# A fused attention and feed-forward kernel: staged loads, V from the padding of K, one GpSimd addition for two, and a forecast that gives VectorE a second tile

## The chip, the cores and the metric

The kernel runs on one core of a Trainium2 chip. The metric is device time in microseconds (us) of one execution; the kernel before takes 809.61 us, the median of 13 runs (808.16 to 811.75). The engines of the core work side by side, each through its own list of instructions in order, and wait for one another by semaphores: TensorE (PE in the profile), VectorE (DVE), ScalarE (ACT), GpSimd (POOL) and SyncE (SP), which here only starts transfers.

## The reference

One transformer layer on 2048 rows of 640 numbers in bf16: attention with 32 query heads of 20 columns that all share one K and one V head, then a gated feed-forward part with 1536 inner columns.

```python
def _A_ref(x, wq, wk, wv, wo):          # x is layernorm(A_x), 2048 x 640
    q = (x @ wq).reshape(B, S, H, Dh)   # then heads first; H = 32, Dh = 20
    k = x @ wk                          # 2048 x 20
    v = x @ wv                          # 2048 x 20
    scores = einsum("bhqd,bkd->bhqk", q, k) * (Dh ** -0.5)
    p = softmax(scores)
    return einsum("bhqk,bkd->bhqd", p, v) (heads joined) @ wo

def _B_ref(x, w_gate, w_up, w_down):    # x is layernorm(h)
    return (gelu(x @ w_gate) * (x @ w_up)) @ w_down

h = x + _A_ref(layernorm(x), ...)
h2 = h + _B_ref(layernorm(h), ...)
```

## The kernel before

**Who decides the order.** The program is written by a planner that runs before anything is emitted. `_Plan.commit` puts an operation at the end of one engine's list, with a planned start, a cost and a latency after which others see its result. The main loop at the end of the kernel takes the engine that is free earliest in planned time and asks that engine's function (`pe_decide`, `act_decide`, `dve_decide`, `pool_decide`, `sp_decide`) for its next operation. Costs and latencies are constants in ns, such as `c_act(n) = n/1.2 + 51` or `POOL_ADD = 635`. They set the order alone: on the chip each engine goes through its finished list, waiting on semaphores where data must come first. An operation that was planned too early therefore holds everything behind it on its engine.

**Scores.** The 2048 query rows are cut into chunks of two tiles of 128 rows (the last two chunks of one), and a chunk into units of several groups of four heads, so that a unit has 512 query columns for each of four heads. For a unit and one tile of 128 keys, `issue_qk` emits a pack: four matmuls, one for each 32-row group of the array, that fill four PSUM banks of 128 x 512 scores. There are 512 packs, 2048 score tiles. A head has 20 columns but takes 32 rows of its group: `wk4` and `wq_pad` hold the weights with 12 zero columns after each 20, so K and the queries carry 12 zero rows, and all four groups of `kT4` hold the same K.

**Exponentials.** `issue_qk` decides how many of the four tiles, `n`, go to DVE; the rest go to ACT. ACT computes the exponential from PSUM into a slot of `pa` (line 1375), one bank (128x512) or two neighbouring banks (128x1024) in one instruction. With n = 1 ACT gets one single and one pair, with n = 2 two singles (since `PAIR2` is 0), with n = 0 two pairs. DVE instead makes a 16-bit number whose bit pattern, read as bf16, approximates the exponential (line 1438). To lower the error it takes three copies of it, of which two are shifted by the integers 42 and 85 (`CH_SHIFT`, the two chord additions), and multiplies each with a V of its own weight (`v_ext`, `CH_W`). So a tile on DVE needs two integer additions and three value matmuls, a tile on ACT one value matmul. The additions wait in `pend[1]` and `pend[2]`; `pool_decide` gives one at a time to POOL (`do_adds`, line 1416), on pairs of 16-bit numbers as int32. DVE may take some too (line 1410), several tiles at once. `pd` has eight slots for such tiles, each with all three copies.

**The rule for n** (line 989): none in the first four packs (`npack`); in a burst, when ACT is planned busy for over 3 us, four or two; none when DVE's planned load `Dv` is over `TH0` = 1500 ns; two when it is under `TH2` = 0, which does not occur; otherwise one.

**Banks.** PSUM has eight. Banks 0 to 5 take scores, bank 6 or 7 holds the unit's accumulated output, and the other serves projections and feed-forward pieces; while no such piece is ready or running, `spare_ok` lends it to scores. Until all K tiles are there (`kv_left`), pieces may also use banks 4 and 5.

**The start.** The loads of x go out from SP, those of wk, wq (two halves) and wv from ACT (line 330). Each tile of x gets its statistics on DVE (line 391), a power on POOL (line 411), a reciprocal and the normalising on DVE (lines 415 and 460), then a transpose: on PE for tiles 0 and 1, by transfer from SP for the others (line 452). `kv_job` then makes K with five accumulating matmuls and V with five more per tile. `flex_copy` tasks take both out of the bank, on DVE or ACT, and free it. POOL copies wk into `wk4` (line 886) and wq into `wq_pad` (`wq_copy`, line 892). A unit's first pack needs its query projection (`q_job`).

**The rest.** Output projection, second layernorm and feed-forward pieces of finished chunks fill PE's gaps between packs, and the last chunk's are the tail.

Of the kernel before, what the change touches and what calls it, by code (L numbers as in the profile page):

```python
# [178 lines left out]
class _Job:  # L179


    __slots__ = ("name", "prio", "pieces", "bank", "then", "seq", "pos", "gate")

    def __init__(self, name, prio, pieces, then, gate=None):
        self.name = name
        self.prio = prio
        self.pieces = pieces
        self.then = then
        self.bank = None
        self.pos = 0  # L190
        self.gate = gate


def bass_sequential_preLN__grouped_kv_mqa__glu_gated_geglu__prompt_kernel(
# [75 lines left out]
    zz = sb("zz", [P, 32], BF16)  # L270
    shifts = sb("shifts", [P, 2], I32)
# [41 lines left out]
    POOL_ADD = 635.0  # L313
    ADD_MIN = 1
# [8 lines left out]
    PAIR2 = 0  # L323
    ADDW = 50.0
# [4 lines left out]
    def load(eng, o, i, key, cost=480.0, lat=2300.0):  # L329
        return plan.commit(eng, (lambda e: e.dma_start(o, i)), cost, lat, writes=key, dma=True)  # L330

    load("sp", xh[:, 0, :], x_view[:, 0, :], [("x", 0)], lat=2000)
    load("act", wk_sb[:], cview(A_wk), ["wk"], lat=2500)
    load("sp", xh[:, 1, :], x_view[:, 1, :], [("x", 1)], lat=2200)
    load("act", wq_stage[:, :, 0:HALF], cview(A_wq)[:, :, 0:HALF], [("wqs", 0)], lat=4000)
    load("sp", xh[:, 2:4, :], x_view[:, 2:4, :], [("x", 2), ("x", 3)], lat=2800)
    load("act", wv_sb[:], cview(A_wv), ["wv"], lat=2500)
    load("sp", xh[:, 4:8, :], x_view[:, 4:8, :], [("x", t) for t in range(4, 8)], lat=4000)
    load("act", wq_stage[:, :, HALF:D], cview(A_wq)[:, :, HALF:D], [("wqs", 1)], lat=4000)
    load("sp", xh[:, 8:12, :], x_view[:, 8:12, :], [("x", t) for t in range(8, 12)], lat=5000)  # L340
    load("sp", xh[:, 12:16, :], x_view[:, 12:16, :], [("x", t) for t in range(12, 16)], lat=6000)
# [40 lines left out]
    def ln_half(ln, t, h, prio, then):  # L382
# [8 lines left out]
        dve(lambda e: e.bn_stats(stats[:, ln, t, 6 * h:6 * h + 6], xh[:, t, h * HALF:(h + 1) * HALF]), 356, [key],  # L391
            [("st", ln, t, h)], prio, c)

    def ln_group(ln, tiles, prio, done):
# [15 lines left out]
        def c3(op):  # L410
            task(("pool",), lambda e: e.tensor_tensor(ln_denb[:, ln, sl], ln_veb[:, ln, sl], halfc[:, 0:n], ALU.pow),  # L411
                 1010, L_POOL, [("veb", kk), "halfc"], [("den", kk)], prio, c4)
# [9 lines left out]
        def norm(t):  # L422
# [33 lines left out]
            tk = _Task(("dve",), None, 310, L_DVE, keys + [("lr", kk)], [], prio, then, gate)  # L456
# [65 lines left out]
    def kv_job(tiles):  # L522
# [3 lines left out]
        for c in range(NC_D):  # L526
            pieces.append((mm(lambda b: bank(b, n), wk4[:, c, :], xn1T[:, c, t0 * P:t0 * P + n],
                              c == 0, c == NC_D - 1), c_mm(n), [("xn1T", t) for t in tiles] + ["wk4"]))
        for i, t in enumerate(tiles):
            for c in range(NC_D):  # L530
                pieces.append((mm((lambda i: lambda b: ps[:, b * 512 + 384 + i * 32:b * 512 + 384 + i * 32 + Dh])(i),
                                  xn1T[:, c, t * P:(t + 1) * P], wv_sb[:, c, :], c == 0, c == NC_D - 1),
                               c_mm(32), [("xn1T", t), "wv"]))

        def then(b):
            cnt = [0]

            def fin(op):
                cnt[0] += 1
                if cnt[0] == 2:  # L540
                    free_bank(b)

            def kfin(op):
# [3 lines left out]
                fin(op)  # L547

            flex_copy(kT4[:, t0 * P:t0 * P + n], bank(b, n), n, [("b", b)], [("k", t) for t in tiles], 0.4, kfin)
            nt = len(tiles)  # L550
            vi = ps[:, b * 512 + 384:b * 512 + 384 + 32 * nt].rearrange("p (t e) -> p t e", t=nt)[:, :, 0:Dh]

            def vfin(op):
                fin(op)
# [330 lines left out]
    wk4v = wk4[:].rearrange("p c (r e) -> p c r e", r=4)[:, :, :, 0:Dh]  # L885
# [762 lines left out]
```

## Time and profile before

| | |
|---|---|
| Median of 13 runs | 809.61 us |
| The profiled execution's own time | 811.45 us |
| Its span (first to last instruction) | 809.7 us |
| ACT busy | 762.0 us (94%) |
| PE busy | 693.3 us (86%) |
| POOL busy | 638.4 us (79%) |
| DVE busy | 573.9 us (71%) |
| Score tiles on DVE | 535 of 2048 |
| Additions on POOL | 1036 |
| First exponential starts | 15.80 us |

In lines of groups, the first number after the bar is the busy time of the group in us, then the mean duration of one in ns, then the idle time of the engine before them and what ended it. In lines of the timeline the first two numbers are start and duration in us, and a bracket gives the idle time before and its releaser. In lines by stretch, the stretch and its length are followed by busy time and number of instructions of PE, weight loads (PEld), DVE, ACT and POOL, then the granted TensorE clock, the share of DMA time and GB/s.

### The profile page before, as it was taken

What the parts mean: (1) busy time and instruction counts of PE and PEld (TensorE: products, weight loads), DVE (VectorE), ACT (ScalarE), POOL (GpSimd) and SP (SyncE); (2) the same over time, 40 slices, a digit from 0 to 9 for tenths busy, and PEclk for the clock granted to TensorE, in tenths of its full rate; (3) what the DMA queues carried; (4) which work ended last, traced back from release to release, by engine and by line L of the source; (5) the groups of instructions that cost most, each with busy time, mean ns of one, the idle gap of its engine ahead of it and who ended that gap; (6) DMA issues with size and microseconds to landing.
All of it is one profiled execution on the core that took longest, in us unless ns stands there. A gap on an engine that the chain in (4) does not pass through costs nothing.

```text
span 809.7 us, 30789 instructions
## 1 busy us (share of the span) xinstructions
PE 693.3 (86%) x13435; PEld 334.2 (41%) x13435; DVE 573.9 (71%) x1060; ACT 762.0 (94%) x1054; POOL 638.4 (79%) x1096
## 2 busy tenths in 40 slices
PE   4777778889889897889978898898988899888998
PEld 2432223444334443345434443354433454344457
DVE  7865557776687766776677766777667766777854
ACT  3699999999999999999999999999999999999991
POOL 5488788888888888888888888888888778888860
PEclk9899999999999999999999999999999999999999
DMA  7590000100100000000000000100000000000000
GB/s 202 81 341 3 2 1 18 20 2 11 25 20 3 2 19 19 19 2 3 18 19 18 2 11 16 29 3 2 19 18 19 2 2 19 19 18 11 11 19 18
DMA packets 40293, 22.01 MB, mean 27 GB/s; under 512 B 31328, under 2 KB 38880, under 8 KB 40160
## 3 DMA queue, kind: packets, MB, share of 16 engines
q1 hardware_dynamic: 37536, 19.18, 9.5%
q8 instruction: 107, 1.75, 0.9%
q10 hardware_dynamic: 2624, 0.87, 0.5%
q14 instruction: 26, 0.21, 0.1%
HBM read 10.21 MB, written 2.62 MB: 16 GB/s over the span
## 4 chain that ended last, share of the span: by engine, by line
ACT 77%; PE 14%; DVE 5%; DMA 2%; issue 1%; POOL 0%; ACTq 0%
ACT pa L1375 73%; PE ps L1037 4%; PE ps L1116 4%; PE ps L498 4%; PE ps L494 3%; DVE pd L1438 2%; ACT gbuf L819 2%; DMA gbuf<-in_A_wq_dram 1%; DVE osb L1143 1%; ACT L1375 1%; ACT L819 1%; DVE xn_tmp L460 1%; DMA xn1T<-xn_tmp 1%; DVE stats L391 0%; PE ps L1240 0%
## 5 line engine op out<-in xcount | busy, mean ns | idle before, releaser
L1375 ACT ACTIVATE pa<-ps 128x512 bf16<-128x512 f32 (+1 forms) x1009 | 713.4, 951 | 17.9 <-PE ps L1037 17.6
L1416 POOL TENSOR_TENSOR pd<-pd,shifts 128x256 int32<-128x256 int32 x1036 | 614.3, 615 | 130.7 <-DVE pd L1438 119.0
L1438 DVE TENSOR_SCALAR pd<-ps 128x512 uint16<-128x512 f32 x535 | 365.5, 689 | 204.8 <-PE ps L1037 198.7
L1116 PE MATMUL ps<-pd,v_ext 128*32 128x512 bf16 x1605 | 274.0, 387 | 34.5 <-DVE osb L1143 18.7
L1116 PE MATMUL ps<-pa,v_ext 128*32 128x512 bf16 x1513 | 265.1, 386 | 3.6 <-DVE pd L1438 2.2
L1037 PE MATMUL ps<-qT,kT 32*128 32x512 bf16 x2048 | 204.4, 384 | 58.3 <-DVE pd L1438 24.8
L1037 PEld LDWEIGHTS ps<-qT,kT 32*128 32x128 bf16 x2048 | 61.0, 91 | 216.2 <-DVE pd L1438 143.0
L1116 PEld LDWEIGHTS ps<-pd,v_ext 128*32 128x32 bf16 x1605 | 73.5, 95 | 94.5 <-ACT pa L1375 32.7
L1116 PEld LDWEIGHTS ps<-pa,v_ext 128*32 128x32 bf16 x1513 | 70.0, 95 | 47.6 <-issue 33.5
L498 PE MATMUL ps<-wd_sb,gbuf 128*32 128x320 bf16 x1344 | 64.1, 301 | 0.0
L498 PE MATMUL ps<-xn2T,wg_sb 128*32 128x256 bf16 (+1 forms) x1748 | 63.4, 272 | 0.7
L498 PE MATMUL ps<-xn2T,wu_sb 128*32 128x256 bf16 x1680 | 61.2, 277 | 2.9 <-DVE gbuf L836 2.9
L498 PEld LDWEIGHTS ps<-xn2T,wg_sb 128*32 128x32 bf16 x1748 | 42.0, 96 | 19.8 <-issue 12.2
L498 PEld LDWEIGHTS ps<-xn2T,wu_sb 128*32 128x32 bf16 x1680 | 41.9, 97 | 18.8 <-issue 9.1
L498 PE MATMUL ps<-xn1T,wq_pad 128*32 128x256 bf16 (+1 forms) x1440 | 47.9, 265 | 0.0
L498 PEld LDWEIGHTS ps<-wd_sb,gbuf 128*32 128x32 bf16 x1344 | 32.9, 96 | 22.8 <-issue 11.1
L498 PEld LDWEIGHTS ps<-xn1T,wq_pad 128*32 128x32 bf16 x1440 | 32.7, 97 | 14.7 <-issue 10.7
L836 DVE TENSOR_TENSOR gbuf<-ps,gbuf 128x512 bf16<-128x512 f32 x48 | 32.7, 682 | 6.6 <-PE ps L494 6.6
L391 DVE BATCH_NORM_STATS2 stats<-xh 128x6 f32<-128x320 bf16 x64 | 30.0, 483 | 3.0 <-DMA xh<-in_A_x_dram 2.6
L799 DVE CAST gbuf<-ps 128x512 bf16<-128x512 f32 x42 | 29.0, 690 | 0.2 <-PE ps L498 0.2
L498 PE MATMUL ps<-wo_sb,onT 128*32 128x320 bf16 x600 | 27.1, 300 | 0.0
L411 POOL TENSOR_TENSOR ln_denb<-ln_veb,halfc 128x2 bf16<-128x2 bf16 (+1 forms) x18 | 12.6, 701 | 15.4 <-DVE ln_veb L407 14.0
(68 smaller groups left out, 334.3 us busy)
## 6 DMA issues: line engine op xcount, KB each, us to landing
out_dram<-xh SPq DMA_DIRECT2D x16, 160.0 KB, 1.8
xh<-in_A_x_dram SPq DMA_DIRECT2D x3, 640.0 KB, 9.5
wg_sb<-in_B_w_gate_dram SPq DMA_DIRECT2D x1, 1920.0 KB, 10.4
wu_sb<-in_B_w_up_dram SPq DMA_DIRECT2D x1, 1920.0 KB, 14.8
wd_sb<-in_B_w_down_dram SPq DMA_DIRECT2D x1, 1920.0 KB, 19.5
gbuf<-in_A_wq_dram ACTq DMA_DIRECT2D x2, 400.0 KB, 9.1
wo_sb<-in_A_wo_dram SPq DMA_DIRECT2D x1, 800.0 KB, 4.9
xh<-in_A_x_dram SPq DMA_DIRECT2D x2, 160.0 KB, 2.8
```

The costliest lines, as they stand in the source:

```text
L391: dve(lambda e: e.bn_stats(stats[:, ln, t, 6 * h:6 * h + 6], xh[:, t, h * HALF:(h + 1) * HALF]), 356, [key], [("st", ln, t, h)], prio, c)
L411: task(("pool",), lambda e: e.tensor_tensor(ln_denb[:, ln, sl], ln_veb[:, ln, sl], halfc[:, 0:n], ALU.pow), 1010, L_POOL, [("veb", kk), "h ...
L494: return e.matmul(o(b), l, r, start=st, stop=sp)
L498: ins = e.matmul(o(b)[a, :], l[:, a], r, start=st, stop=sp, tile_position=(0, 32 * j))
L799: dve(lambda e: e.tensor_copy(o, i), c_dve(n * k), [("b", bk)], ks, 1.0, fin)
L819: task(("act",), (lambda v: lambda e: e.activation(v, v, ACT.Gelu_apprx_tanh))(v), ("gelu", c_act(n * (f1 - f0))), L_ACT, ks, ks, 1.0, (la ...
L836: dve(lambda e: e.tensor_tensor(o, i, o, ALU.mult), c_dve(n * k), [("b", bk)] + ks, ks, 1.0, fin)
L1037: ins = e.matmul(bank(b), kT4[32 * r:32 * r + 32, kt * P:(kt + 1) * P], qT[32 * r:32 * r + 32, s, :], start=True, stop=True, tile_position ...
L1116: ins = e.matmul(ps[32 * r:32 * r + 32, ab * 512:(ab + 1) * 512], v_ext[:, it["kt"], it["w"], :], it["ap"], start=st, stop=(j in ends), ti ...
L1375: op = plan.commit("act", lambda e: e.activation(dst, src, ACT.Exp, scale=SM_SCALE), cost, L_ACT, [("b", b0 + i) for i in range(n)], [("pa ...
L1416: return e.tensor_tensor(pd32[:, w, h], pd32[:, 0, h], shifts[:, w - 1:w].to_broadcast([P, 256 * k]), ALU.add)
L1438: op = plan.commit("dve", lambda e: e.tensor_scalar(pd[:, 0, s * 512:(s + 1) * 512], bank(b), CH_A, CH_B, ALU.mult, ALU.add), c_dve(512), ...
```

## The change

There are four parts and some new constants.

1. *Loads.* `load` can wait for earlier data. SP now starts x tile 0, x tile 1 and wv; then, when tile 0 has landed, x tiles 2 and 3, 4 to 7, 8 to 11, the second half of wq, and x tiles 12 to 15. ACT starts wk and the first half of wq. The planned landing times are later than before. A wq copy may go to ACT while no pack has been issued.
2. *V from the padding rows.* POOL copies the 20 columns of wv, 10 and 10, into the zero columns of the first two 32-column groups of `wk4`. The K projection then brings V, transposed, in rows 20 to 29 of those groups of `kT4`. The query's rows are zero there, so the scores do not change. After the K copy, one matmul for each tile with `vsel` (columns 20 to 29 and 52 to 61 of the identity) takes V out into the same bank, transposed back. The five V matmuls of a tile are gone. `wk4` is now ready only when both wk and wv have come.
3. *Both additions at once.* When the same slot stands first in `pend[1]` and `pend[2]`, POOL adds both shifts in one instruction (`add_both`) on 2 x 256 int32 numbers.
4. *Two tiles to DVE.* n is also 2 if DVE's load is under 400 ns, fewer than six additions wait, and `stall` forecasts that the pack with n = 2 leaves ACT ready more than 300 ns earlier than with n = 1. `stall` sorts the times at which banks come free, from the ACT and DVE queues with the new pack added, takes the one that makes the fourth bank free and compares the next pack's arrival with the end of ACT's work.

The constants `HEADN`, `HEAD2` and `NP0` leave the conditions in which they stand as they were. The planned costs of statistics, normalising and the power change from 356, 310 and 1010 to 395, 420 and 780.

```diff
+    POOL_ADD2 = 1200.0
+    SP2 = 1
+    SP2D = 400.0
+    SP2P = 3
+    SP2G = 300.0
...
+    load("sp", xh[:, 0, :], x_view[:, 0, :], [("x", 0)], 2000)
+    load("act", wk_sb[:], cview(A_wk), ["wk"], 2500)
+    load("sp", xh[:, 1, :], x_view[:, 1, :], [("x", 1)], 2300)
+    load("act", wq_stage[:, :, 0:HALF], cview(A_wq)[:, :, 0:HALF], [("wqs", 0)], 4500)
+    load("sp", wv_sb[:], cview(A_wv), ["wv"], 3000)
+
+    load("sp", xh[:, 2:4, :], x_view[:, 2:4, :], [("x", 2), ("x", 3)], 3200, [("x", 0)])
+    load("sp", xh[:, 4:8, :], x_view[:, 4:8, :], [("x", t) for t in range(4, 8)], 5800)
+    load("sp", xh[:, 8:12, :], x_view[:, 8:12, :], [("x", t) for t in range(8, 12)], 8500)
+    load("sp", wq_stage[:, :, HALF:D], cview(A_wq)[:, :, HALF:D], [("wqs", 1)], 10000)
+    load("sp", xh[:, 12:16, :], x_view[:, 12:16, :], [("x", t) for t in range(12, 16)], 12800)
...
-        for i, t in enumerate(tiles):
-            for c in range(NC_D):
-                pieces.append((mm((lambda i: lambda b: ps[:, b * 512 + 384 + i * 32:b * 512 + 384 + i * 32 + Dh])(i),
-                                  xn1T[:, c, t * P:(t + 1) * P], wv_sb[:, c, :], c == 0, c == NC_D - 1),
-                               c_mm(32), [("xn1T", t), "wv"]))
...
+                jb = _Job(("v", t0), 0.5, vpieces, vthen)
+                jb.bank = b
+                bank_owner[b] = jb.name
+                active.append(jb)
...
+            vpieces.append((mm((lambda i: lambda b: ps[:, b * 512 + i * 32:b * 512 + i * 32 + Dh])(i),
+                               kT4[:, t * P:(t + 1) * P], vsel[:], True, True), c_mm(32), [("k", t), "vsel"]))
...
+    ptask(lambda e: e.tensor_copy(wk4r[:, :, 0:2, Dh:Dh + VH], wv_sb[:].rearrange("p c (r e) -> p c r e", r=2)), 160,
+          ["wv", "wk4z"], ["wk4v"], 1.05)
...
+    def stall(t, n, fb):
+
+        free = [t] * (len(fb) - 4)
+        ta = plan.free["act"]
+        for kind, tl in act_q:
+            ta = max(ta, tl[0]["vis"]) + c_act(512 * len(tl))
+            free += [ta + L_ACT] * len(tl)
+        td = plan.free["dve"]
+        for x in dve_q:
+            td = max(td, x["vis"]) + 600.0
+            free.append(td + L_DVE)
+        free += [r for r, b in free_banks(t)[1] if b not in fb]
+        vis = t + 445.0
+        ta = max(ta, vis)
+        for k in ((2, 2), (1, 2), (1, 1))[n]:
+            ta += c_act(512 * k)
+            free += [ta + L_ACT] * k
+        td = max(td, vis)
+        for _ in range(n):
+            td += 600.0
+            free.append(td + L_DVE)
+        free.sort()
+        return max(0.0, free[3] + 460.0 - ta)
...
-        elif Dv < TH2:
+        elif Dv < TH2 or (SP2 and Dv < SP2D and len(pend[1]) + len(pend[2]) < 2 * SP2P
+                          and stall(t, 1, fb) + 1382.0 - stall(t, 2, fb) - 956.0 > SP2G):
             n = 2
...
+    def add_both(t):
+
+        x = pend[1].pop(0)
+        y = pend[2].pop(0)
+        s = x["slot"]
+        h = slice(s * 256, (s + 1) * 256)
+
+        def fn(e):
+            return e.tensor_tensor(pd32[:, 1:3, h], pd32[:, 0, h].unsqueeze(1).to_broadcast([P, 2, 256]),
+                                   shifts[:].unsqueeze(2).to_broadcast([P, 2, 256]), ALU.add)
+        op = plan.commit("pool", fn, POOL_ADD2, L_POOL, [("pd", 0, s), ("sh", 1), ("sh", 2)],
+                         [("pd", 1, s), ("pd", 2, s)], at=t)
+        x["add"](1, op)
+        y["add"](2, op)
...
+            if pend[1] and pend[2] and pend[1][0]["slot"] == pend[2][0]["slot"] and pend[1][0]["at"] <= t + 20:
+                add_both(t)
+                return True
```

## The prediction

> **What bounds the kernel now.** I read the page's busy shares first, then the chain of waits, then busy time by stage, then the costliest groups, and last the start in the timeline. The page's first part and the lines by share of the chain:
>
> ```profile
> PE 693.3 (86%) x13435; PEld 334.2 (41%) x13435; DVE 573.9 (71%) x1060; ACT 762.0 (94%) x1054; POOL 638.4 (79%) x1096
> ACT 77%; PE 14%; DVE 5%; DMA 2%; issue 1%; POOL 0%; ACTq 0%
> ```
>
> ScalarE is busiest and carries 77% of the chain, 73% of it exponentials. An average hides stages, so the next view is busy time in four stretches (columns: PE, PEld, DVE, ACT, POOL):
>
> ```profile
> 0.00:15.80 15.80, 5.24 (x143) 3.84 (x147) 11.25 (x41) 3.85 (x8) 8.87 (x28) 1.00 0.89 240
> 15.80:40.00 24.20, 17.14 (x532) 10.57 (x524) 20.96 (x72) 15.64 (x18) 11.94 (x25) 0.86 0.55 80
> 40.00:785.00 745.00, 649.06 (x12471) 300.94 (x12469) 532.02 (x926) 735.75 (x1019) 617.00 (x1044) 1.00 0.08 21
> 785.00:809.70 24.70, 21.83 (x302) 18.86 (x299) 9.66 (x21) 6.76 (x10) 0.62 (x2) 1.00 0.04 15
> ```
>
> From 40 to 785 us ACT is idle for 9 us only: there time is won only by taking exponentials off ACT. Before 40 us ACT is idle for 20.5 us (12.0 before the first exponential at 15.80, 8.6 after it): there earlier data wins time. The tail is dependent work that the change does not touch. The groups that the rest is priced from (mean ns of one; idle before it and its releaser):
>
> ```profile
> L1416 POOL TENSOR_TENSOR pd<-pd,shifts 128x256 int32<-128x256 int32 x1036 | 614.3, 615 | 130.7 <-DVE pd L1438 119.0 <-DVE ln_r L415 2.0
> L1375 ACT ACTIVATE pa<-ps 128x1024 bf16<-128x1024 f32 x504 | 587.9, 1168 | 4.3 <-PE ps L1037 4.3
> L1375 ACT ACTIVATE pa<-ps 128x512 bf16<-128x512 f32 x505 | 369.8, 735 | 13.6 <-PE ps L1037 13.4
> L1438 DVE TENSOR_SCALAR pd<-ps 128x512 uint16<-128x512 f32 x535 | 365.5, 689 | 204.8 <-PE ps L1037 198.7
> ```
>
> Of 2048 score tiles DVE takes 535. DVE and POOL stand idle for 199 and 119 us waiting for the next score pack, not for lack of capacity. A mean ACTIVATE overlaps its neighbours, so I take pitches: in the chain 60 ACTIVATEs (30 packs of one single and one pair) take 41.89 us, 1.396 us a pack; two pairs take 1.94 us and four 3.77, so a pair is 0.915 and a single 0.481.
>
> The start, on POOL and DVE (bracket: idle before and releaser):
>
> ```profile
> 3.21 0.89 DVE L391 BATCH_NORM_STATS2 stats<-xh 128x6 f32<-128x320 bf16 x2 [1.01 <-DMA xh<-in_A_x_dram]
> 5.65 0.55 POOL L411 TENSOR_TENSOR ln_denb<-ln_veb,halfc 128x1 bf16<-128x1 bf16 x1 [1.56 <-DVE ln_veb L407]
> 6.91 0.49 DVE L391 BATCH_NORM_STATS2 stats<-xh 128x6 f32<-128x320 bf16 x1 [1.35 <-DMA xh<-in_A_x_dram]
> 8.04 0.52 POOL L892 COPY wq_pad<-gbuf 128x400 bf16<-128x400 bf16 x1 [1.84 <-DMA gbuf<-in_A_wq_dram]
> 8.62 0.14 DVE L415 RECIPROCAL ln_r<-ln_denb 128x1 f32<-128x1 bf16 x1
> 13.88 0.98 POOL L892 COPY wq_pad<-gbuf 128x400 bf16<-128x400 bf16 x2 [1.96 <-DMA gbuf<-in_A_wq_dram]
> wv_sb<-in_A_wv_dram ACTq DMA_DIRECT2D x1, 25.0 KB, 8.7
> ```
>
> The power for tile 0 is done at 6.20, but its reciprocal runs at 8.62: the written-out order put statistics of tiles 2 and 3 ahead of it, whose data came at 6.9. The power for tile 1 stood behind a wq copy whose data came at 8.04 (it ran at 8.51). Loads later than forecast hold the in-order engines.
>
> [...] the 25 KB of wv needed 8.7 us among the x and wq loads while wk, first in its queue, needed 2.7. [...] the pitches give 0.915 - 0.481 = 0.434.
>
> **The change part by part.**
>
> *Two tiles to DVE.* A pack now costs ACT single + pair, 1.396 us; with two tiles on DVE it costs two singles, 0.962. One moved tile is worth 0.43 us of ACT. When does the rule fire? It asks for DVE load under 400 ns, fewer than six pending additions and a forecast gain over 300 ns, that is an added ACT stall under 126 ns. I work this with the plan's own times for a pack in which six banks hold scores. Let ACT's backlog be A when the pack issues. The old pair's two banks come free at A + 310, DVE's first at 445 + 600 + 150 = 1195, ACT's first new single at A + 478 + 310 = A + 788; the next pack needs the fourth of these, so its tiles arrive at A + 788 + 460 while ACT runs dry at A + 956: stall 292, over 126, and no move. With a seventh bank the fourth is the 1195, and the move is allowed once A exceeds 573. So it fires only where bank 6 or 7 is lent to scores, which `spare_ok` allows when no projection or feed-forward piece is ready. Counted over the timeline's PE rows, 138 of 512 packs have no such matmul from 0.3 us before to 1.1 us after their start, about 54 of these before 147 us, where feed-forward work begins. A unit has 16 packs; its first and last three or so are barred (two open units, or fewer than three tiles left): 138 x 10/16 = 86 eligible.
>
> How many of the 86? POOL alone allows a share f with (1 + f) x 1.18 = 1.396 - 0.43 f: f = 0.13, 11 tiles. If DVE, with about 0.7 us free a pack, takes the surplus additions (eight single ones averaged 278 ns), it is full near f = 0.45, 39 tiles. I take 22. Of the 0.43 I deduct 0.12 for the stall that the rule tolerates: 22 x 0.31 = 6.8 us. Ends: 0 and 39 x 0.43 = 16.8. A moved tile adds two value matmuls; eight take 0.60 us where four take 0.39, so 0.05 each, 22 x 0.11 = 2.4 us, hidden in PE's 96 us of idle in the stretch. It adds 0.6 us to DVE (13 us in 213) and 1.18 to POOL (26 in 128 idle).
>
> *Both additions in one instruction.* Today two take 1.18 us end to end. [...] The first addition becomes visible 0.57 us later, the second not; only value matmuls wait for it, and 16 exponential slots stand between those and ACT.
>
> *Loads.* The third x load now waits on SP for tile 0 (landed at 3.2, issued today at 1.65), and x4 to 7, x8 to 11, the second half of wq and x12 to 15 stand behind it on SP; no other SP work is due before the transposes at 12.39. It lets tile 1, wk, wv and the first wq half through first: wq half one should land near 6 instead of 8.04. x2 and x3 should land at about 7, as now. wv moves from 10.5 to 5 or 6, and must, for the K matmuls now need it. Chain, tile 1: statistics ended at 5.3; aggregate, cast and add to 6.0, power to 6.6, reciprocal and normalising to 7.4, where today it normalises at 10.58 to 11.0. Allow 0.5 for order: the first exponential moves from 15.80 to about 12.7, 3.1 us. ACT then runs at its duty of 15.64/24.20 = 65%: 2.0 us.
>
> *V from the padding rows.* Removed: 320 matmuls of 20 columns and their loads; the runs of 20 take 0.28 to 0.44 us, 16 x 0.35 = 5.6 us of PE before 45 us. Added: a K = 128 selection per tile, 16 x 0.1 = 1.6. PE is idle for 7 of 24 us there, so it earns little: I take 0.5 us. Against it: V waits for the K copy, so its bank is held longer by about a matmul and a copy (0.7 us, nine times), while ACT's 8.6 us of idle there comes from few free banks: I take -0.4. The two small POOL copies and the wq copies that ACT may now take cost nothing: ACT is idle from 4.65 to 10.06.
>
> *Forecast numbers* (statistics 395, normalising 420, power 780) change order alone; they lie nearer the measured 440 pitch, 400 and 550 to 760. Zero, -1 to +1.
>
> Sum: 6.8 + 2.0 + 0.5 - 0.4 = 8.9 us. The profiled execution took 811.45 us (span 809.7); the median is 809.61, 1.84 less. 811.45 - 8.9 = 802.6 profiled, **800.7 as a median**.
>
> **Rivals.** (1) The head only: the rule hardly fires, because banks are seldom spare; 809.6 - 2.1 for the head - 0.4 for a tile or two = about 807. For it: packs follow a DVE release within 0.1 us from 200 us on. Chance 0.16. (2) Many moves: DVE takes additions readily and shorter periods open more gaps: 45 to 60 tiles x 0.4 plus the head, 785 to 790. For it: DVE's 199 us of waiting. Against: six pending additions cap it. Chance 0.12. (3) Slower: the double addition, with its broadcast inputs and three-dimensional pattern that no row shows, takes much longer than 1.23. From the first addition to the last, POOL has 753 us, less 11 of other work: for 555 tiles it decides at 742/555 = 1.34 us. At 1.40 POOL needs 777 + 11 and the time is about 809.6 + 35 = 845. [...] Chance 0.08. (4) No change: bank holding and reordering eat the head, and the few moves nothing: 809.6. Chance 0.08, half of it a little on either side. The main case, 0.56, spans 794 to 806.
>
> Faster by over 0.2% (about what a measurement of this kernel can tell from no change, 1.6 us): 0.56 + 0.15 + 0.12 = 0.83; within 0.2%: 0.07; slower: 0.10. Range 787 to 811: rival 2's lower half and rival 3 stay outside.
>
> **What would show it.** Right: DVE evictions 545 to 575 (535 now), ACT singles up and pairs down by one for each move, moves gathered before 150 us; [...] first exponential at 12 to 13.5 us; no POOL wait for wv beyond 6 us; ACT still over 98% busy from 40 us on. Wrong: ACT idle in the middle growing past 15 us, POOL busy over 95%, evictions under 540 or over 580, or a first exponential not earlier.

## The result and the profile after

The changed kernel takes **805.43 us** (median of 11 runs, 804.23 to 807.19), the kernel before 809.65 (median of 48 runs): ratio 0.9948 [0.9936, 0.9959], a gain of 4.2 us. The forecast was 8.9. The profiled execution took 806.89 us, its span is 805.1.

The page of the changed kernel: busy time, the chain by engine, and two groups of instructions. Line 1423 is now the exponential, 1509 the VectorE evictions, 1486 the double addition.

```profile
PE 693.7 (86%) x13162; PEld 332.3 (41%) x13162; DVE 627.4 (78%) x1156; ACT 750.2 (93%) x1065; POOL 585.8 (73%) x624
...
PE 42%; ACT 32%; DVE 22%; issue 2%; DMA 1%; POOL 1%; POOLq 0%; DVEq 0%
...
L1486 POOL TENSOR_TENSOR pd<-pd,shifts 128x512 int32<-128x512 int32 x517 | 534.1, 1041 | 169.9 <-DVE pd L1509 165.2
L1509 DVE TENSOR_SCALAR pd<-ps 128x512 uint16<-128x512 f32 x587 | 395.1, 687 | 143.1 <-PE ps L1083 132.4
```

DVE takes 587 tiles instead of 535, and a double addition lasts 1.04 us, less than the 1.18 that two single ones took end to end. ACT's share of the chain fell from 77% to 32%: the chain now leaves ACT often, for score packs that wait on PE and DVE. The same in stretches (busy PE, PEld, DVE, ACT, POOL, then granted clock, DMA share, GB/s):

```profile
0.00:14.56 14.56, 5.92 (x122) 4.17 (x126) 10.04 (x36) 5.52 (x11) 6.55 (x24) 1.00 0.87 250
14.56:40.00 25.44, 18.87 (x344) 9.09 (x337) 22.08 (x73) 20.49 (x29) 13.02 (x24) 0.80 0.59 98
40.00:780.00 740.00, 646.63 (x12392) 299.68 (x12394) 584.90 (x1026) 718.53 (x1019) 565.67 (x576) 0.97 0.08 21
780.00:805.10 25.10, 22.28 (x319) 19.35 (x312) 10.35 (x22) 5.67 (x9) 0.56 (x1) 1.00 0.05 15
```

Before 40 us ACT is busy for 26.0 us instead of 19.5. In the middle it is now idle for 21.5 us of 740, where it was 9: more than the 15 that the prediction named as a sign of being wrong.

**Where the time went.** I add up ACT's work from the start of score pack 20 to the end of the last exponential. Where exponentials follow one another without a gap, a pair starts 0.904 us after the one before it and a single 0.477. GELUs and table loads take some 38 us in every kernel here; what remains, to within 0.7 us, is waiting.

| | before | after |
|---|---|---|
| score pack 20 starts | 56.56 us | 54.30 us |
| pairs, singles | 479, 490 | 426, 544 |
| exponentials at those pitches | 666.7 us | 644.6 us |
| waits of ACT | 22.7 us | 41.9 us |
| last exponential ends | 784.84 us | 779.38 us |
| from there to the end of the span | 24.9 us | 25.7 us |

So 2.3 us were won at the start and 22.1 on exponentials; 19.2 were lost to new waits and 0.8 in the tail: 4.4 by these sums, 4.6 by the spans (809.7 and 805.1). The experiments ask where the 19.2 come from.

### The profile page after: what moved, and what is told of

The parts are those of the page before. It is cut to its first block, busy times and chain, and to the rows that moved or that the text cites. A ratio compares the mean times of both kernels' runs of the same rounds, so it can differ in the third digit from the quotient of the medians.

```text
span 805.1 us, 29858 instructions
## 1 busy us (share of the span) xinstructions
PE 693.7 (86%) x13162; PEld 332.3 (41%) x13162; DVE 627.4 (78%) x1156; ACT 750.2 (93%) x1065; POOL 585.8 (73%) x624
## 4 chain that ended last, share of the span: by engine, by line
PE 42%; ACT 32%; DVE 22%; issue 2%; DMA 1%; POOL 1%; POOLq 0%; DVEq 0%
ACT pa L1423 30%; PE ps L510 15%; DVE pd L1509 13%; PE ps L1083 12%; PE ps L1162 11%; PE ps L506 3%; DVE pd L1466 2%; DVE xn_tmp L472 2%; DVE osb L1189 1%; DVE stats L403 1%; ACT gbuf L829 1%; DVE qT L580 1%; DVE xh L728 1%; DMA onT<-onq 1%; DVE onq L668 0%
## 5 line engine op out<-in xcount | busy, mean ns | idle before, releaser
L1423 ACT ACTIVATE pa<-ps 128x512 bf16<-128x512 f32 (+1 forms) x1012 | 699.0, 851 | 26.3 <-PE ps L1083 21.4
L1486 POOL TENSOR_TENSOR pd<-pd,shifts 128x512 int32<-128x512 int32 x517 | 534.1, 1041 | 169.9 <-DVE pd L1509 165.2
L1509 DVE TENSOR_SCALAR pd<-ps 128x512 uint16<-128x512 f32 x587 | 395.1, 687 | 143.1 <-PE ps L1083 132.4
L1162 PE MATMUL ps<-pd,v_ext 128*32 128x512 bf16 x1761 | 274.1, 396 | 28.3 <-DVE osb L1189 21.5
L1083 PE MATMUL ps<-qT,kT 32*128 32x512 bf16 x2048 | 206.7, 390 | 66.1 <-DVE pd L1509 40.7
L1083 PEld LDWEIGHTS ps<-qT,kT 32*128 32x128 bf16 x2048 | 59.0, 91 | 234.7 <-DVE pd L1509 163.6
L1162 PEld LDWEIGHTS ps<-pa,v_ext 128*32 128x32 bf16 x1461 | 70.4, 96 | 41.9 <-issue 29.2
L510 PE MATMUL ps<-xn2T,wu_sb 128*32 128x256 bf16 x1680 | 65.7, 279 | 0.0
L510 PE MATMUL ps<-xn2T,wg_sb 128*32 128x256 bf16 (+1 forms) x1720 | 65.4, 277 | 0.1
L510 PE MATMUL ps<-xn1T,wq_pad 128*32 128x256 bf16 (+1 forms) x1440 | 50.9, 266 | 0.1
L510 PEld LDWEIGHTS ps<-xn2T,wg_sb 128*32 128x32 bf16 x1720 | 41.9, 97 | 17.2 <-issue 11.1
L1466 DVE TENSOR_SCALAR pd<-pd 128x512 uint16<-128x512 uint16 (+2 forms) x66 | 37.6, 591 | 0.0
L1472 POOL TENSOR_TENSOR pd<-pd,shifts 128x256 int32<-128x256 int32 x48 | 30.2, 635 | 4.2 <-DVE pd L1509 3.7
L510 PE MATMUL ps<-wo_sb,onT 128*32 128x320 bf16 x600 | 28.5, 301 | 0.7 <-DMA onT<-onq 0.4
## 6 DMA issues: line engine op xcount, KB each, us to landing
wd_sb<-in_B_w_down_dram SPq DMA_DIRECT2D x1, 1920.0 KB, 18.1
```

Of the source, the lines that this page charges most:

```text
L510: ins = e.matmul(o(b)[a, :], l[:, a], r, start=st, stop=sp, tile_position=(0, 32 * j))
L1083: ins = e.matmul(bank(b), kT4[32 * r:32 * r + 32, kt * P:(kt + 1) * P], qT[32 * r:32 * r + 32, s, :], start=True, stop=True, tile_position ...
L1162: ins = e.matmul(ps[32 * r:32 * r + 32, ab * 512:(ab + 1) * 512], v_ext[:, it["kt"], it["w"], :], it["ap"], start=st, stop=(j in ends), ti ...
L1423: op = plan.commit("act", lambda e: e.activation(dst, src, ACT.Exp, scale=SM_SCALE), cost, L_ACT, [("b", b0 + i) for i in range(n)], [("pa ...
L1466: return e.tensor_scalar(pd[:, w, a], pd[:, 0, a], float(CH_SHIFT[w]), None, ALU.add)
L1472: return e.tensor_tensor(pd32[:, w, h], pd32[:, 0, h], shifts[:, w - 1:w].to_broadcast([P, 256 * k]), ALU.add)
```

## The experiments

Line numbers are those of the changed kernel. "Waits" are those of the table above, of one profiled execution, which can lie up to 2.7 us off its kernel's median (797.13 against 799.83 for the fastest kernel), so small differences of waits are not to be read closely. "Clock" is the granted TensorE clock, averaged over a kernel's executions. A ratio is to the kernel before run beside that kernel; in these groups of runs its median was 809.2 to 809.8.

| kernel | median us | ratio to before, 95% | tiles on DVE | waits us | clock |
|---|---|---|---|---|---|
| before | 809.65 | 1 | 535 | 22.7 | 0.993 |
| after | 805.43 | 0.9948 [0.9936, 0.9959] | 587 | 41.9 | 0.972 |
| loads, V, costs only | 804.92 | 0.9936 [0.9920, 0.9952] | 537 | 22.3 | 0.989 |
| + double addition | 814.78 | 1.0067 [1.0052, 1.0082] | 532 | 29.4 | 0.989 |
| + moves, single additions | 805.75 | 0.9954 [0.9937, 0.9971] | 583 | 30.4 | 0.980 |
| after, moves in the first 84 packs only | 810.17 | 1.0004 [0.9991, 1.0017] | 549 | 31.0 | 0.983 |
| double addition as two halves, no moves | 815.43 | 1.0067 [1.0048, 1.0086] | 532 | 29.8 | 0.984 |
| after, double addition as two halves | 802.58 | 0.9910 [0.9893, 0.9926] | 587 | 38.4 | 0.973 |
| moves, single additions, weight loads held | **799.83** | 0.9879 [0.9855, 0.9902] | 583 | 31.8 | 0.984 |
| before + planned costs | 813.40 | 1.0050 [1.0031, 1.0070] | 539 | 28.5 | 0.986 |
| before + loads | 808.37 | 0.9990 [0.9978, 1.0002] | 535 | 25.5 | 0.992 |
| halves, each shown when done, no moves | 816.01 | 1.0080 [1.0060, 1.0101] | 532 | 28.8 | 0.984 |
| the same with moves, weight loads held | 803.58 | 0.9918 [0.9901, 0.9934] | 590 | 37.4 | 0.984 |
| loads, V, costs only; single planned at 600 | 807.39 | 0.9967 [0.9955, 0.9979] | 537 | 24.2 | 0.989 |
| double addition planned at 1270, no moves | 814.99 | 1.0066 [1.0045, 1.0086] | 532 | 29.4 | 0.987 |

### Which part does what

Four kernels take the change apart: neither moves nor double addition; double addition without moves; moves without double addition; and moves only before feed-forward work begins. The expectations of these runs weigh two ideas. The outcome given first belongs to the idea that DVE's work on SBUF data ends late beside a long addition on POOL: normalising takes 684 ns on average in the changed kernel, 531 before. The second idea is called tile theory here, and visibility theory in the two runs further on that issue the same plan with halves.

```diff
# neither moves nor double addition
-    SP2 = 1
+    SP2 = 0
-            if pend[1] and pend[2] and ...
+            if False and pend[1] and pend[2] and ...
```

> The changed kernel without the rule for two tiles and without the double addition: loads, V from the padding rows and the new planned costs alone. [...] normalising stays at its old mean of about 530 to 560 ns. Tile theory (the second eviction of a pack itself makes the next pack late, whatever GpSimd does): no difference to before after 50 us. Both: the early part alone is worth 2 to 4 us, 805.5 to 807.5.

```diff
# double addition, no moves
-    SP2 = 1
+    SP2 = 0
```

> The changed kernel without the rule for two tiles; the double addition stays. [...] normalising keeps a mean over 680 ns with a maximum near 1.2 us, and the time is 1 to 3 us above the run without double additions. Tile theory: within 1 us of the run without double additions, and ScalarE's lateness after 160 us is back at that of the kernel before.

```diff
# moves, single additions
-            if pend[1] and pend[2] and ...
+            if False and pend[1] and pend[2] and ...
```

> The changed kernel with the rule for two tiles, but with each chord addition in its own GpSimd instruction; the plan has 583 evictions and about 100 additions on VectorE (66 before). [...] normalising back at about 560 ns, single additions on VectorE near 280 to 350 ns, 800 to 803 us. Tile theory: as much lateness of ScalarE as in the changed kernel, 805 to 808 us.

```diff
# moves in the first 84 packs only
-        elif Dv < TH2 or (SP2 and Dv < SP2D and ...
+        elif Dv < TH2 or (SP2 and state["npack"] < 84 and Dv < SP2D and ...
```

> The changed kernel, with the rule for two tiles allowed only in the first 84 of 512 packs (before the feed-forward work begins); the plan has 549 evictions. The lead over the kernel before at pack 84 should be about 6.9 us as in the changed kernel. [...] part of it is lost later to stretched normalising, 803 to 805 us. Tile theory: it is kept, 801.5 to 803.5 us.

Loads, V and costs together give 4.7 us, over twice the 2.1 that I gave them. Adding the double addition alone makes the kernel 9.9 us slower than that (814.78 against 804.92), which no theory of mine had. With single additions the moves bring nothing (805.75), for a reason that a later section finds at the start. With the double addition the moves take 9.35 us off again (814.78 to 805.43). And -4.7 + 9.9 - 9.35 is the measured gain. This is one way to split it: taken out of the changed kernel instead, the double addition costs nothing (805.75 against 805.43). The early moves alone give 4.6 of the 9.35. But the rule goes on firing while feed-forward work runs: of the 52 additional tiles 15 come before pack 84 and 37 after it.

### The double addition without moves: length, order or planned cost?

POOL is not short of time (its group waits 204.5 us for DVE in this kernel), so I tested three causes: that the instruction is one long piece, that the first sum is shown late (other engines learn only at the end that it is done), and that the planned cost of 1200 differs from two times 635. In the first kernel the same plan issues two half instructions, of which the second signals for both; in the second each half is planned at 600 and signals when it is done; in the third the pair is planned at 1270; in the fourth the kernel without pairing plans a single one at 600.

```diff
# the same plan, two halves (SP2 = 0)
-            return e.tensor_tensor(pd32[:, 1:3, h], pd32[:, 0, h].unsqueeze(1).to_broadcast([P, 2, 256]), ...
+            for w in (1, 2):
+                ins = e.tensor_tensor(pd32[:, w, h], pd32[:, 0, h], shifts[:, w - 1:w].to_broadcast([P, 256]), ALU.add)
+            return ins
```

> The run without moves that kept the double addition (814.8 us), with the same plan and the same order on every engine, but the double addition issued as two instructions of 256 numbers, the second alone telling that both are done. [...] normalising falls from a mean of 703 ns to about 500, and most of the 10 us comes back, 805 to 808 us. Visibility theory (the first addition is seen later, so value matmuls and buffers come late): no gain, since both are still seen at the end; 813 to 816 us.

```diff
# each half planned and shown by itself (SP2 = 0; fn adds copy w)
-        op = plan.commit("pool", fn, POOL_ADD2, L_POOL, ...
-        x["add"](1, op)
-        y["add"](2, op)
+        for w, z in ((1, x), (2, y)):
+            z["add"](w, plan.commit("pool", fn, POOL_ADD2 / 2, L_POOL, [("pd", 0, s), ("sh", w)], [("pd", w, s)], at=t))
```

> The split run without moves (815.4 us), with the two halves of the pair planned and signalled one by one, 600 ns each, so that value matmuls may use the first addition half a pair earlier, in the plan and on the chip. Visibility theory (seeing both additions only at the end of the pair delays value matmuls, above all where a unit ends and its accumulator must be emptied): ScalarE's waits at unit ends shrink and 804 to 808 us. Order theory (the loss comes from pairing the additions and from the order that follows, not from when they are seen): 813 to 816 us.

```diff
# SP2 = 0
-    POOL_ADD2 = 1200.0
+    POOL_ADD2 = 1270.0
```

> The double addition without the rule (814.8 us), planned at 1270 ns, as long as two single ones are planned. Planned-cost theory: waits after pack 20 fall from 29 to about 22 us, 804 to 808 us. Pairing theory: 812 to 816 us. A third reading, that any new order of this plan moves the time by several us either way, would show as a value that fits neither.

```diff
# SP2 = 0, no double addition
-    POOL_ADD = 635.0
+    POOL_ADD = 600.0
```

> The early part alone (single additions, no rule; 804.9 us) with one number changed: a single addition is planned at 600 ns instead of 635, which is nearer to the measured pitch of 593 and equals half of the 1200 planned for the pair. Planned-cost theory (the paired runs lose because the plan believes GpSimd 70 ns faster per tile and packs the order at unit ends more tightly): ScalarE's waits after pack 20 rise from 22 to about 29 us, 812 to 816 us. Pairing theory (taking both additions of one tile together is what makes the worse order): 804 to 807 us.

All four kernels with pairing lie at 814.8 to 816.0; the single additions at the lower planned cost lie at 807.4. So neither length nor visibility nor the price in the plan makes the 10 us. Between the two profiled executions with and without the double addition lie 11.0 us: 7.1 of waits, 2.4 of exponentials (532 tiles on DVE instead of 537), 0.9 before pack 20 and 0.6 in the tail. What remains as the cause is that POOL takes both additions of a tile in a row, after which the plan comes out in another order. The four paired kernels have nearly the same order, though (on ACT at least 1048 of 1062 instructions stand in the same place), and count as one case rather than four: this order is slow, but that pairing leads to slow orders elsewhere is not shown. A kernel that pairs nothing can be as slow: before with other planned costs takes 813.40.

Where this order loses is seen at the ends of units, where DVE copies the accumulator out (line 1189) and PE's value matmuls (1162) wait for that, with the next score pack (1083) behind them on PE. The timeline of one such end in the kernel with the double addition and no moves (start, duration; bracket: idle before and releaser):

```profile
194.63 0.69 DVE L1509 TENSOR_SCALAR pd<-ps 128x512 uint16<-128x512 f32 x1 [0.71 <-PE ps L1083]
195.24 0.68 DVE L1189 CAST osb<-ps 128x512 bf16<-128x512 f32 x1
195.98 0.39 PE L1162 MATMUL ps<-pd,v_ext 128*32 128x512 bf16 x1 [0.52 <-DVE osb L1189]
196.31 0.39 PE L1083 MATMUL ps<-qT,kT 32*128 32x512 bf16 x4
196.76 2.00 ACT L1423 ACTIVATE pa<-ps 128x512 bf16<-128x512 f32 x3 [0.39 <-PE ps L1083]
```

And an end in the kernel with neither:

```profile
192.06 0.40 PE L1083 MATMUL ps<-qT,kT 32*128 32x512 bf16 x4
192.16 0.69 DVE L1189 CAST osb<-ps 128x512 bf16<-128x512 f32 x1 [0.30 <-PE ps L1162]
192.90 0.39 PE L1162 MATMUL ps<-pd,v_ext 128*32 128x512 bf16 x1 [0.20 <-DVE osb L1189]
193.59 0.40 PE L1083 MATMUL ps<-qT,kT 32*128 32x512 bf16 x4
```

Here a pack is sent ahead of the copy, and ACT does not stop; there the copy stands behind an eviction, the pack behind both, and ACT waits 0.39 us. It is no single case. PE's waits of line 1162 for 1189, without and with the double addition (total us, times, longest):

```profile
PE ps L1162 <- DVE osb L1189: 15.0, 18, 1.4
PE ps L1162 <- DVE osb L1189: 25.2, 26, 3.1
```

The six pack intervals around each emptying average 9.48 and 9.51 us in the two kernels of this early part with single additions, and 9.75 to 9.80 in the four that pair without moves. Over 30 unit ends that is 7 to 10 us, most of the difference. Single additions do not ensure short ends, however: the kernel before, alone or with the new loads or costs, has 9.58 to 9.65. Why the planner comes to the slower order with pairing I did not find out; it stays open.

### The double addition with moves: a long instruction that delays DVE

With moves, the plan of the changed kernel was issued with the halves. In the second kernel each half is shown when done, and weight loads are held as in a later section.

```diff
# two halves as in the first kernel of the part above, with SP2 = 1
-            return e.tensor_tensor(pd32[:, 1:3, h], ...
+            for w in (1, 2):
+                ins = e.tensor_tensor(pd32[:, w, h], ...
+            return ins
```

> The changed kernel (805.4 us), plan and order unchanged, with the double addition issued as two instructions. [...] single additions on VectorE fall from 496 ns to about 350, normalising from 684 to about 560, and 796 to 800 us. Visibility theory: 804 to 807 us.

```diff
# each half shown by itself, SP2 = 1
-      lambda: plan.free["sp"] > 30000.0
+      lambda: plan.free["sp"] > 30000.0 and len(x1_done) == NT
```

> The same pairs, seen one by one, with the rule for two tiles and with the weight loads held until the transposes are issued; 590 evictions, 70 additions on VectorE. Visibility theory: at or below the 799.8 us of the run with single additions and held loads, 796 to 800 us[...]. Order theory: 802 to 806 us.

The order of all instructions is that of the changed kernel, at nearly the same clock (0.973 and 0.972), and yet the halves, which need more POOL time in all (605.2 us against 534.1), are 2.9 us faster: 802.58 against 805.43, intervals apart. That lies between the two expectations, so less came back than the first idea said. Groups by shape of the changed kernel:

```profile
L1423 ACT ACTIVATE pa<-ps 128x1024 bf16<-128x1024 f32 x449 | 488.1, 1090 | 3.4 <-PE ps L1083 3.3
L1423 ACT ACTIVATE pa<-ps 128x512 bf16<-128x512 f32 x563 | 358.5, 660 | 22.8 <-PE ps L1083 18.1 <-PE ps L1162 0.2
...
L472 DVE TENSOR_SCALAR xn_tmp<-xh,mv,ln_r 128x640 bf16<-128x640 bf16 x32 | 21.4, 684 | 0.4
L1466 DVE TENSOR_SCALAR pd<-pd 128x512 uint16<-128x512 uint16 x43 | 21.1, 496 | 0.0
```

Of the kernel before:

```profile
L460 DVE TENSOR_SCALAR xn_tmp<-xh,mv,ln_r 128x640 bf16<-128x640 bf16 x32 | 15.8, 531 | 0.1
...
L1410 DVE TENSOR_SCALAR pd<-pd 128x512 uint16<-128x512 uint16 x8 | 2.2, 278 | 0.0
```

Of the changed kernel's plan with halves:

```profile
L1487 POOL TENSOR_TENSOR pd<-pd,shifts 128x256 int32<-128x256 int32 x1034 | 605.2, 613 | 98.3 <-DVE pd L1510 87.2 <-PE ps L510 4.0 <-DVE ln_veb L419 1.1
...
L1466 DVE TENSOR_SCALAR pd<-pd 128x512 uint16<-128x512 uint16 x43 | 18.8, 444 | 0.0
L472 DVE TENSOR_SCALAR xn_tmp<-xh,mv,ln_r 128x640 bf16<-128x640 bf16 x32 | 16.6, 535 | 0.4
```

A normalising instruction takes 684 ns on average beside the long additions and 535 beside the halves, where undisturbed ones take 0.42 to 0.45 us; a DVE addition 496 and 444. The evictions, which read PSUM, do not change (687 and 688). The timeline of the changed kernel shows what that does:

```profile
233.45 1.04 POOL L1486 TENSOR_TENSOR pd<-pd,shifts 128x512 int32<-128x512 int32 x1 [0.18 <-DVE ln_r L427]
233.48 1.19 DVE L472 TENSOR_SCALAR xn_tmp<-xh,mv,ln_r 128x640 bf16<-128x640 bf16 x1
234.59 0.68 DVE L1509 TENSOR_SCALAR pd<-ps 128x512 uint16<-128x512 f32 x1
...
235.35 1.04 POOL L1486 TENSOR_TENSOR pd<-pd,shifts 128x512 int32<-128x512 int32 x1 [0.86 <-DVE pd L1509]
235.36 1.21 DVE L472 TENSOR_SCALAR xn_tmp<-xh,mv,ln_r 128x640 bf16<-128x640 bf16 x1
...
236.96 0.67 DVE L1509 TENSOR_SCALAR pd<-ps 128x512 uint16<-128x512 f32 x1
...
237.78 0.40 PE L1083 MATMUL ps<-qT,kT 32*128 32x512 bf16 x4 [1.73 <-DVE pd L1509]
238.22 1.08 ACT L1423 ACTIVATE pa<-ps 128x512 bf16<-128x512 f32 x2 [0.94 <-PE ps L1083]
```

Twice a normalising that starts just after an addition ends only 0.18 us after the addition has ended (1.19 and 1.21 us long). The eviction behind the second one comes late, its bank comes free late, the score pack waits 1.73 us and ACT 0.94. It goes the other way too: six additions in this trace that start about 0.16 us into a normalising last 1.17 us instead of 1.04. Run wholly one after the other, from 1.04 and 0.43 us, such an addition would end after 1.31 us and such a normalising after 1.44 (estimate from these durations): the measured ones are 0.14 and 0.23 to 0.25 us shorter. So in both directions the one that starts later is drawn out; what couples the two is not shown. Without moves the halves gain nothing (815.43 against 814.78), although normalising falls there too, from 653 to 542 ns: such a delay need not cost time by itself.

The second kernel takes 803.58 us, no better than the halves shown together. It is no clean test of visibility, since its order is another one, its weight loads are held, and 30.4 us pass in it from the last exponential to the end of the span, 4.5 more than with the halves shown together; earlier signals show no gain as a whole, and what they are worth alone stays open.

### The granted clock

Kernels with moves run at a granted clock of 0.972 to 0.984, those without at 0.984 to 0.993, and the changed kernel at the lowest. Its stretches around the GELUs at 256 to 262 us (columns as above):

```profile
254.00:258.00 4.00, 3.88 (x94) 2.31 (x86) 3.27 (x6) 3.97 (x6) 3.23 (x4) 1.00 0.00 0
258.00:262.00 4.00, 1.04 (x17) 0.29 (x16) 4.00 (x7) 3.98 (x4) 2.63 (x3) 1.00 0.03 6
262.00:266.00 4.00, 3.60 (x52) 1.21 (x44) 1.75 (x5) 4.00 (x6) 0.57 (x1) 0.59 0.00 0
266.00:270.00 4.00, 4.00 (x64) 1.88 (x60) 2.48 (x4) 2.61 (x5) 2.99 (x4) 0.56 0.02 4
270.00:274.00 4.00, 4.00 (x96) 2.25 (x96) 2.86 (x5) 3.88 (x7) 2.86 (x4) 1.00 0.00 0
```

And at the same GELUs in the kernel with neither moves nor double addition:

```profile
255.00:259.00 4.00, 3.40 (x37) 1.07 (x29) 4.00 (x8) 3.98 (x4) 4.00 (x8) 1.00 0.01 4
259.00:263.00 4.00, 2.10 (x34) 0.76 (x33) 3.64 (x7) 3.73 (x6) 2.74 (x5) 1.00 0.00 0
263.00:267.00 4.00, 3.20 (x72) 1.61 (x68) 2.79 (x6) 4.00 (x7) 3.52 (x7) 1.00 0.00 0
```

While ACT does its GELUs, PE falls to 1.04 us busy in 4 in the first kernel and to 2.10 in the second. In the first the clock then drops to half for some seven microseconds, PE cannot feed ACT, and ACT is idle for 1.4 us of the four from 266 on. The traces of before and after give the clock as 1 or 0.5, and every stretch between two changes of it is a whole multiple of 3.41 us, from one (a drop of 3.41 us) to 178; the drops of the changed kernel after 40 us last 3.41 or 6.83 us. So I laid out windows of 3.41 us on the times at which the clock changes, in all fifteen traces from 45 to 780 us, with PE busy as the trace models it. All 35 windows at full clock in which PE was busy for less than 45% were followed by a drop, 23 of 104 at 45 to 61%, and none of 2977 above. (In the traces of before and after alone it is 5 of 5, 4 of 13 and none of 398.) PE was not idle in those of the changed kernel: it was busy for 24 to 41% of each of its four.

Counted from 40 us, the changed kernel has eight drops, with 9.1 of its 21.5 us of ACT idle in them and the microsecond after; the kernel before two, with 1.3 of 9.1; double addition without moves two, with 2.1 of 13.9. Moves are not the only way to them: before with other planned costs has six.

What does a drop cost? The executions of one kernel, the same program, differ in clock. Over 12 executions of the changed kernel (0.968 to 0.977) a line through them gives 2.7 us for each 0.01; the same line gives 0.6 to 5.8 in the other kernels, so this is a rough price. From 0.993 to 0.972 that is 5.7 us against the kernel before, and 4.6 of the 12.5 us of waits that the moves add (29.4 to 41.9); by the idle time in the drops, 7.0. This is a correlation and a few traces, not an experiment: no kernel was run with PE kept busy through the GELUs, and waits that come from elsewhere can also make PE quiet. Moves close by are not needed for PE to fall quiet, for the kernel whose moves end with pack 84, at about 140 us, has four drops after 250 us.

### Moves with single additions, and a collision at the start

Moves with single additions gave 805.75, no better than no moves (804.92), though waits rose by only 8.1 us for 18.1 us of exponentials saved. The loss lies before pack 20, which starts at 60.90 us instead of 52.60. ACT's timeline there, then SyncE's queue:

```profile
54.07 0.38 ACT L579 ACTIVATE kT<-ps 128x256 bf16<-128x256 f32 x1 [7.35 <-PE ps L510]
```

```profile
35.31 0.58 SPq L924 DMA_DIRECT2D wo_sb<-in_A_wo_dram  x1
35.94 0.52 SPq L924 DMA_DIRECT2D wg_sb<-in_B_w_gate_dram  x1
36.50 0.53 SPq L924 DMA_DIRECT2D wu_sb<-in_B_w_up_dram  x1
40.23 7.97 SPq L464 DMA_TRANSPOSE xn1T<-xn_tmp  x2
```

In this plan three loads of weights, due much later, go out just before the last two transposes of x. A transpose then took up to 11.7 us to land (median 2.6), K of the last tiles came late, and ACT stood for 7.35 us. I held those loads until all transposes are planned:

```diff
# single additions as above, and
-      lambda: plan.free["sp"] > 30000.0
+      lambda: plan.free["sp"] > 30000.0 and len(x1_done) == NT
```

> The rule for two tiles with single additions (805.75 us), and the loads of the output and feed-forward weights held until all 14 transposes of the first layernorm are issued. In the run without this, three of these loads went ahead of the last two transposes, a transpose then needed up to 11.7 us to land, and ScalarE waited 7.35 us for K. If that was an accident of this plan, 8 us come back and the moves show their worth: 796 to 799 us. If the moves are worth nothing with single additions, 804 to 807 us.

799.83 us, 5.9 less, and the fastest kernel of all: ratio 0.9879 [0.9855, 0.9902]. No transpose now takes longer than 5.0 us to land. The time is 5.6 us below the changed kernel's; what held loads alone would bring to the changed kernel was not run. Pack 20 starts at 52.61. Its page:

```profile
PE 693.5 (87%) x13165; PEld 333.8 (42%) x13165; DVE 621.4 (78%) x1187; ACT 748.2 (94%) x1063; POOL 639.7 (80%) x1098
```

Against the kernel with neither moves nor double addition, 46 more tiles on DVE save 18.1 us of exponentials and cost 9.5 us of waits, 0.21 each. That profiled execution is 2.7 us faster than its kernel's median and the other 0.7 faster; if the rest is waits, it is 0.25 each (estimate). With single additions POOL is at 80%, and in the trace of the kernel whose loads are not held no wait of ACT is put down to it.

### The start: loads and planned costs

```diff
# before, with the planned costs of after only
-  bn_stats ... 356     +  395
-  power ... 1010       +  780
-  normalising ... 310  +  420
```

> The kernel before with only the three planned costs changed (statistics 395, normalising 420, power 780). The prediction took these for nothing (-1 to +1 us). If they are the cause of the slow gain of 3 us that the run without rule and double addition makes after 60 us, 806 to 808 us; if loads and V carry the whole of the early part, 809 to 810.5 us.

In the other kernel the one edit is that the kernel before gets after's loads (its `load` and the ten lines of loads in the diff of the change).

> The kernel before with the new loads and their planned landing times alone. The prediction gave them 2.0 us: 807 to 808.5 us. If the 4.85 us of the early part hang on the loads, 804.5 to 806 us; if they need the planned costs or V from the padding rows with them, 808.5 us or more.

The loads alone bring pack 20 forward by 3.5 us, yet the kernel is only 1.3 us faster, within what can be told from no change: the plan that follows has 2.8 us more waits. The three costs alone make it 3.8 us slower, with 5.8 us more waits and a tail 1.7 us longer, at 2.4 us less of exponentials. Loads, costs and V together give the 4.7; V was not run by itself. The parts do not add up, since every edit makes the planner order all that follows anew; plans without moves or pairing differ by up to 6 us in waits and 8.5 us in time.

## Why the prediction was right or wrong

The median lies in the range, and the sign was right, but the gain was 4.2 us, not 8.9.

**Both additions in one instruction: the step that failed.** I costed it at nothing, an estimate that no trace of before showed, with POOL's 119 us of waiting as cover. The instruction is even shorter (1.04 us) than the 1.18 that two took. But on the kernel without moves pairing costs 9.9 us, through an order of the unit ends that halves, earlier signals and another planned cost leave nearly as it is; why that order arises stays open. With moves, where the order is another one, the long instruction itself costs 2.9 us (805.43 against 802.58), with normalising beside it at 684 ns instead of 535. I had priced the instruction by its own engine and never asked what it delays.

**Two tiles to DVE: right mechanism, both terms too small.** The price of a moved tile held: 0.904 - 0.477 = 0.427 against 0.43. But 52 tiles moved, not 22 (587 is outside my 545 to 575), since the rule fires during feed-forward work too. They were not gathered before 150 us either: 37 of the 52 came after pack 84. And each brought 0.21 to 0.25 us of new waits rather than 0.12: 12.5 for 52 to 55 tiles with double additions, 9.5 or more for 46 with single ones. I took only the stall that the rule tolerates, not the normalising that additions draw out (up to 1.21 us); the lower clock may have its part in this, which is not shown. Net -9.35 us instead of -6.8. My count of eligible packs from the matmul rows was the weak part, and rival 2, with its 45 to 60 tiles, had the count right and the price of a move wrong.

**Loads: earlier, as said, but by less.** After's start in the timeline:

```profile
6.32 1.39 ACT L911 ACTIVATE wq_pad<-gbuf 128x400 bf16<-128x400 bf16 x3 [3.03 <-DMA gbuf<-in_A_wq_dram]
6.47 0.27 POOL L900 COPY wk<-wv_sb 128x100 bf16<-128x100 bf16 x1 [2.23 <-DMA wv_sb<-in_A_wv_dram]
6.71 1.07 POOL L423 TENSOR_TENSOR ln_denb<-ln_veb,halfc 128x1 bf16<-128x1 bf16 x2
7.29 0.16 DVE L427 RECIPROCAL ln_r<-ln_denb 128x1 f32<-128x1 bf16 x1 [1.61 <-POOL ln_denb L423]
8.28 0.14 DVE L427 RECIPROCAL ln_r<-ln_denb 128x1 f32<-128x1 bf16 x1
8.73 0.42 DVE L472 TENSOR_SCALAR xn_tmp<-xh,mv,ln_r 128x640 bf16<-128x640 bf16 x1
13.12 0.60 ACT L579 ACTIVATE qT<-ps 128x512 bf16<-128x512 f32 x1 [1.51 <-PE ps L510]
14.56 2.92 ACT L1423 ACTIVATE pa<-ps 128x1024 bf16<-128x1024 f32 x4 [0.63 <-PE ps L1083]
```

The first wq half landed near 6.3 (forecast 6), wv at 6.47, half a microsecond past the bound I had set. I had taken the small POOL copies for nothing. But the copy of wv stands ahead of both powers in POOL's list and held POOL for 2.23 us: the powers ran from 6.71, though their inputs were done by 5.7. So the reciprocal at 7.29 is only that of tile 0. That of tile 1 ran at 8.28, and its normalising ended at 9.15, not 7.4. The first exponential started at 14.56, not 12.7: of the 3.1 us 1.24 were won. Most of what made up for it came before 40 us: ACT's duty from the first exponential to 40 us is 20.49/25.44 = 81%, not the 65% that I carried over. By pack 20 the kernel with these parts alone is 4.0 us ahead, the changed kernel 2.3.

**Forecast numbers.** "Zero, -1 to +1" was wrong for these alone: +3.8 us.

**Rivals.** Rival 3, the slower one, asked for an instruction above 1.34 us; the slowdown exists, without that. Rival 1 comes nearest in its time (807), but not in its reason, for the rule fires often. The two signs that I had named for a failure, ACT idle over 15 us in the middle and evictions over 580, both came.

With single additions and the weight loads held, the gain was 9.8 us, near the forecast; that is not how I had come by the number, since there the larger head and a dearer, larger number of moves happen to make up the sum.

## What to carry to other kernels

Price a merged instruction by what it delays on other engines and by the order that it brings about, and test it against two halves in the same plan: that alone showed the chip's share (2.9 us with moves, none without) apart from what comes with the plan. Where a planner writes the order, any edit orders all that follows anew, by several us here; count work at measured pitches and waits apart, before a gain or a loss is put down to an edit. Look for lulls of PE as well as for waits: in the traces here, a window of 3.41 us with PE under 45% busy was followed by half clock each time (35 of 35).

## What the runs showed of the hardware that I had not expected

- The addition with broadcast inputs takes 1.04 us for 512 int32 elements where 256 take 0.613: 1.67 ns for each further element, so that by this slope some 185 ns of a 0.613 us addition do not grow with the elements (estimate from these two durations).
- A normalising instruction of 128x640 averages 684 ns beside 1.04 us additions and 535 beside 0.61 us ones, with single cases of 1.21, and about 0.43 undisturbed. An operation on 128x2 numbers took up to 1.03 us (changed kernel, at 134.2 us) instead of 0.17.
- The clock fell from 1 to 0.5 after every window of 3.41 us with PE under 45% busy (35 of 35), after some at 45 to 61% (23 of 104) and after none above (0 of 2977). A kernel's executions differ by up to 0.013 in mean clock, in the changed kernel at some 2.7 us for each 0.01.
- A transpose by transfer behind three weight loads landed after up to 11.7 us instead of 2.6.
